# Reordering the first retention segment and splitting a mask-table load in a fused retention and SwiGLU kernel

## The chip, the cores and the metric

The kernel runs on one core of a Trainium2 chip. The metric is device time in microseconds (us) for one execution, given as the median of several runs. A core has a matmul engine (PE, its weight loads are PEld), a vector engine (DVE), a scalar engine (ACT), a Pool engine (POOL) and a queue engine (SP) that here issues all the DMAs. Each engine works through its own list of instructions in the order in which the program gives them, and semaphores make one engine wait for another.

## The reference

A retention layer is followed by a SwiGLU feed-forward block. There are 4 sequences of 768 positions, 8 heads, and 64 columns to a head.

```
state = gamma[h] * state + outer(k[t], v[t])        # for each sequence and head
y[t]  = scale * q[t] @ state
x     = y with heads side by side                    # 3072 x 512
out   = (silu(x @ w_gate) * (x @ w_val)) @ w_out     # 512 -> 1536 -> 512
```

The weights arrive in double precision and are turned into single precision on the chip.

## The kernel before, in words

The retention is computed in chunks of 128 positions. Inside a chunk, the scores k.q are multiplied by a table of decays (the mask) and then by v; what came earlier enters through a small state matrix. Four segments of 768 tokens each (three chunks of two sequences) pass through the feed-forward block: an up stage of 12 column blocks f (products with the gate and value weights, arranged as seven products of half-size blocks instead of eight), then a down stage.

The first segment is special. Its retention (six chunks, numbered 0 to 5 in the order in which they are handled) is the first thing that the kernel does, and it happens while the first weights are loaded and converted. The order of this part is written out by hand in a string, START (line 291), and `do` (line 284) walks through it: each word calls one helper, and each helper appends instructions to the lists of the engines that it uses. A word is a letter, a chunk or piece number, and sometimes a part:

- `l n:w` loads array w (0 is k transposed, 1 is q transposed, 2 is v, 3 is k) of chunk n, 256 KB (line 143). `A n` loads a part of the table of masks and decays (line 277; the parts are in `tabs`, line 977).
- `s n` makes the scores of chunk n on PE into banks 4 and 5 (line 418), and then multiplies them by the mask on DVE into a buffer (line 424). All six chunks use these two banks, so the scores of one chunk wait until the mask operations of the one before have read them.
- `k n`, `q n` scale k and q by decays on POOL (lines 437 and 432); capital `K n`, `Q n` do it on DVE.
- `t n` is the state product on PE (line 458), followed by a copy on ACT (line 461) or an addition on DVE (line 463). `g n` decays a state on ACT (line 444).
- `m n` mixes: products of q with the state (line 475) and of the masked scores with v (line 478) on PE, and a copy to `first` on ACT (line 481). Chunks 0 and 1 have no state yet and so only the second half.
- `x j:i` are sums of pairs of chunk outputs on DVE (line 80, called from line 633), needed by the seven-product scheme. `T n:i` are the corresponding sums of weights.
- `w n` issues n products of zeros on PE (line 963), whose result nobody reads.
- `U n:p` loads weight piece n in double precision, 1 MB for a pair of gate and value blocks (line 191), into the staging buffer `rawp` number p/2. `a n`, `b n`, `c n` are the three ACT parts of its conversion (lines 209, 213, 217), `S n` the DVE part (line 223), `C n` the POOL part (line 232), which frees the staging buffer. Piece 0 has its POOL part in two halves.

A DMA that must wait (for its buffer, or for the landing of the DMA eight places before it) waits on SP, and all DMAs behind it in the list wait with it. Two such waits matter here. U2 goes into the buffer of piece 0 and has to wait for C0. U3 goes into the buffer that holds k and q of chunk 5, so it has to wait for q5, and for m5 on PE.

After START, `up(f)` (line 653) issues the seven products of a block (line 663), with a list `beside` of further conversions between them. The down stages follow, `h_split` (line 851) taking its offsets from a table WHEN. Segments 1 to 3 take their products from lines 824 and 874.

Of the kernel before, what the change touches and what calls it, by code (L numbers as in the profile page):

```python
# [24 lines left out]
NF = DFF // P  # L25
# [10 lines left out]
MASK0, QDEC0, KDEC0, GDEC0 = 0, 2 * NP * P, 3 * NP * P, 3 * NP * P + H  # L36
NTAB = GDEC0 + NP
# [12 lines left out]
def tile_retnet_swiglu(  # L50
# [69 lines left out]
    def at(t, fn, *args, **kw):  # L120
        events.append((t, len(events), lambda: fn(*args, **kw)))
# [23 lines left out]
    def seg_chunks(s):  # L145
        p, pos = divmod(s * L, NCK)
        return [(2 * p + i) * NCK + pos + j for j in range(L) for i in range(2)]
# [136 lines left out]
    def do(order):  # L284
# [4 lines left out]


    START = """
        l0:0 l0:1 A0 l1:0 l1:1 l0:2 l1:2 A1 l0:3 l2:0 l2:1 l1:3 l2:2 l2:3 l3:0 l3:1 l3:2
        l3:3 l4:0 l4:1 U0:0 l4:2 l5:0 l5:1 l5:2 l4:3 l5:3 s1 s0 K0 m1 w6 k2 K1 t0 m0 s2 t1
        g3 Q2 g2 x0:0 x0:1 s3 U1:2 q3 m2 m3 t2 x1:0 k3 a0 x0:2 x0:3 t3 b0 x1:1 s4 S0 q4 x1:2
        c0 s5 q5 x1:3 m4 C0 m5 a1 x2:0 U3:4 T0:0 x2:1 T0:1 U2:0 T0:2 x2:2 x2:3 U12:6
    """
    beside = """
        b1 | c1 S1 U13:7 | g5 g4 C1 | a2 T1:0 U14:8 | U15:9 | c2 b2 T1:1 a3 |
# [26 lines left out]
    WHEN = {  # L325
        ('u', 0): (1.15, 2.19, 2.89, 3.24, 4.29, 5.33, 6.38, 7.08, 7.43, 8.13),
        ('u', 1): (1.15, 2.19, 2.89, 3.24, 4.29, 5.33, 6.38, 7.08, 7.43, 8.13),
        ('u', 2): (1.15, 2.19, 2.89, 3.24, 4.29, 5.33, 6.38, 7.08, 7.43, 8.13),
        ('u', 3): (1.15, 2.19, 2.89, 3.24, 4.29, 5.33, 6.38, 7.08, 7.43, 8.13),
        ('w', 0, 0): (-9.0, -7.4, -6.2),  # L330
        ('w', 0, 1): (-9.0, -7.4, -6.2),
        ('w', 0, 2): (-9.0, -7.4, -6.2),
        ('w', 1, 0): (-7.2, -5.6, -4.4),
# [14 lines left out]
        ('h', 9): (-7.5, -6.3, -5.3),  # L348
        ('h', 10): (-7.5, -6.3, -5.3),
        ('h', 11): (-7.5, -6.3, -5.3),  # L350
        ('s', 0, 0): (0.0, 0.0),
        ('s', 0, 1): (0.0, 0.0, 0.0, 0.0),
        ('m', 0): (0.0, 0.0, 0.0),
# [31 lines left out]
    UP0, T0 = 9.45, 18.0  # L385
# [323 lines left out]
    def item(kind, n):  # L709
        k = turns[kind]  # L710
        turns[kind] += 1
        slots = {"g": 4, "o": 3}[kind]
        t = place(f"{kind}item{k}", {"g": 3 * 2 * TH, "o": 3 * DM}[kind], R12,
                  tag=f"{kind}{k % slots}")
        return t[:, : 3 * n].rearrange("p (a b) -> p a b", a=3)

    def near_a(o, x):
        act(o[0], x, AF.Copy, scale=CUT / FAR)  # L718

    def near_b(o, x):  # L720
        stt(o[1], f32(o[0]), -FAR, x, op0=mul, op1=add)  # L721

    def near_c(o, op=pool):
        op(o[2], f32(o[0]), f32(o[1]), op=add)  # L724
# [52 lines left out]
    def make_x(t, s, p):  # L777
        for m, d in enumerate(WHEN["sum", p]):
            at(t + d, sum_x, m)
        for n in range(3):  # L780
            for d, step in zip(WHEN["far", p, n], (
                    lambda n=n: far_a(*x_part(s, p, n)), lambda n=n: far_b(*x_part(s, p, n)),
                    lambda n=n: far_c(x_part(s, p, n)[0]), lambda n=n: far_d(x_part(s, p, n)[0]))):
                at(t + d, step)
# [63 lines left out]

    hs, wo = {}, {}

    def h_split(t, f):
        it = {}

        def begin():
            hs[f] = item("g", 2 * TH)
            it["o"] = [hs[f][:, i] for i in range(3)]
            near_a(it["o"], hT[:, f].rearrange("p i t -> p (i t)"))

        a, b, c = WHEN["h", f]
        at(t + a, begin)  # L860
        at(t + b, lambda: near_b(it["o"], hT[:, f].rearrange("p i t -> p (i t)")))
        at(t + c, lambda: near_c(it["o"], both))

    def w_load(t, f):
        def load():
            wo[f] = item("o", DM)
            nc.sync.dma_start(out=wo[f].bitcast(U32), in_=w_dn3[f])

        at(t - 8.0, load)
# [31 lines left out]
    def down_stage(s, t, first_order=range(6), between=None):  # L901
        nxt = s + 1 if s + 1 < NSEG else None
        slot_at, steps = [], []
        for n in range(6 * NF):
            f, b = divmod(n, 6)
            slot_at.append(t)
            if b == 0:
                steps.append(t)
            if nxt and n in PARTS:
                what, p, g = PARTS[n]  # L910
                ci = seg_chunks(nxt)[2 * p] % NCK
                d = t + COST[what] + 0.1
                if what == "s":
                    at(t, scores_of, p, g)
                    w = WHEN["s", p, g]
                    for i in range(2):
                        at(d + w[i], decayed, p, g, i)
                    if g and ci:
                        for i in range(2):
                            at(d + w[2 + i], scale_q2, p, i)  # L920
                elif what == "m":
                    at(t, mix_own, nxt, p)
                    w = WHEN["m", p]
                    at(d + w[0], fence)
                    if ci < NCK - 1:
                        for i in range(2):
                            at(d + w[1 + i], scale_k2, p, i)
                elif what == "o":
                    at(t, mix_other, nxt, p)
                    if p == 0:  # L930
                        at(t, begin_x, nxt)
                    for k, w in enumerate(WHEN["y", p]):
                        at(d + w, bring_y, k % 2, k // 2 % 2, k // 4)
                    if ci < NCK - 1:
                        at(d + WHEN["old", p], decay2, nxt, p)
                    make_x(d, nxt, p)
                elif ci < NCK - 1:
                    at(t, state2, nxt, p)
                    at(d + WHEN["new", p], keep_state, nxt, p)
                t += COST[what]  # L940
            tok = (first_order if f == 0 else range(6))[b]
            at(t, down, f, tok)
            t += 3 * PASS_D
            if f == NF - 1:
                at(t + WHEN["end" if nxt else "last"][tok], finish, s, tok)
            if between and n == 0:
                at(t, between)
                t += 1.0
        for f in range(NF):
            h_split(steps[f], f)  # L950
            if s or f > 2:
                w_load(steps[f], f)
        if nxt:
            for n, h in LOADS.items():
                at(slot_at[h] + 1.0, load_pair, nxt, n)
            for f in range(3):
                at(slot_at[UNITS[f]], load_unit, f)
        return t
# [15 lines left out]
    early = [flat[:, ts(i, 512)] for i in range(18)] + [  # L974
        hsp[:, ts(i % 4, 512)] for i in range(6)]

    tabs = slice(0, QDEC0), slice(QDEC0, NTAB)
    early[20:22] = early[18:20]
    early[18:20] = [chunk_x[:, ts(i, 512)] for i in (2, 3)]
    early[22:] = [chunk_x[:, ts(i, 512)] for i in (0, 1)]  # L980
# [8 lines left out]
    for n in range(3, 5):  # L989
        at(end + 1.0 + n, load_pair, 1, n)  # L990
    t = down_stage(0, end, (0, 4, 3, 2, 5, 1), last_gates)
    for s in range(1, NSEG):
        for f in range(NF):
            up3(s, f, t + UPT * f)
            if f > 2:
                at(t + UPT * (f - 1) - 2.5, load_unit, f)
        t += NF * UPT
        if s + 1 < NSEG:
            for n in range(5):
                at(t - (18, 13, 12, 5, 4)[n], load_pair, s + 1, n)  # L1000
        t = down_stage(s, t)
# [52 lines left out]
```

## Time and profile before

| | before |
|---|---|
| runs (us) | 695.98, 696.91, 695.15; median 695.98 |
| the profiled execution, its own time | 693.57 us |
| its span | 691.8 us |
| PE busy from 0 to 9.03 us | 3.78 us |
| PE busy from 14.50 to 36.57 us (retention) | 20.27 of 22.07 us |
| PE busy from 36.57 to 86.15 us (up stage, first part) | 46.36 of 49.58 us |
| PE busy from 86.15 to 150.00 us (up stage, the rest) | 63.85 of 63.85 us |
| the rest, 150.00 to 691.80 us | 527.16 of 541.80 us |

The profile is of one execution, so its times are held against 693.57 us and not against the median. Its span is 1.8 us shorter than the time. A line of the timeline gives start and duration in us, the engine, the line of the kernel, the operation, what it writes and reads, and a count; in brackets stands the idle time of the engine before it and what ended it. A matmul in single precision shows as two instructions, so the 8 products of a chunk's scores are "x16".

### The profile page before, as it was taken

The page shows a single profiled execution, that of the slowest core. Times are in us where ns is not written, and L with a number is a line of the kernel's source. Part 1 is how long each engine was busy: PE and PEld are TensorE (multiplying, and loading weights), DVE is VectorE, ACT ScalarE, POOL GpSimd, SP SyncE. Part 2 cuts the span into 40 slices and gives each one's busy share as a digit, 9 for nine tenths or more (in the row PEclk, how much of TensorE's full clock was granted, in tenths as well). Part 3 has the DMA queues.
Part 4 walks back from the last instruction along what each step waited for, and adds up shares of the span by engine and source line. Part 5 has one row for each costly group of instructions (what it writes and reads, how often), then busy time and mean ns, then how long its engine had stood idle before and what let it go on. Part 6 is the DMA issues. An engine that isn't in the chain of part 4 may idle for free.

```text
span 691.8 us, 12321 instructions
## 1 busy us (share of the span) xinstructions
PE 666.2 (96%) x4724; PEld 551.0 (80%) x4724; DVE 474.9 (69%) x742; ACT 382.5 (55%) x793; POOL 250.3 (36%) x164
## 2 busy tenths in 40 slices
PE   6899899999999999999999999999999999999997
PEld 5755455567678899997777899998777799999885
DVE  2558998985887766665777767666577867667541
ACT  1488879755556454553578555554464645555111
POOL 0334557640112666640110665661011465562000
PEclk9999999999999999999999999999999999999999
DMA  8689899966574543364756433264756453313553
GB/s 316 230 309 335 313 328 400 397 226 216 202 253 169 196 146 107 132 217 162 249 203 220 170 137 116 98 205 168 232 180 213 194 190 126 140 54 119 196 188 136
DMA packets 49578, 141.58 MB, mean 205 GB/s; under 512 B 6128, under 2 KB 18928, under 8 KB 49520
## 3 DMA queue, kind: packets, MB, share of 16 engines
q1 hardware_dynamic: 49520, 140.80, 58.6%
q8 instruction: 37, 0.61, 0.3%
q14 instruction: 21, 0.17, 0.1%
HBM read 114.04 MB, written 26.74 MB: 204 GB/s over the span
## 4 chain that ended last, share of the span: by engine, by line
PE 64%; DVE 17%; ACT 9%; issue 4%; DMA 3%; SPq 1%; POOL 0%; DVEq 0%; ACTq 0%; POOLq 0%
PE bank L824 34%; PE bank L874 14%; PE bank L663 9%; PE bank L520 4%; ACT chunk_x L759 4%; DVE gitem L721 3%; DVE x L733 2%; DVE x L80 2%; DMA rawp<-in_w_gate_dram 2%; DVE tmp L80 1%; DVE gitem L80 1%; PE bank L418 1%; ACT gitem L718 1%; DVE chunk_x L885 1%; DVE tmp L539 1%
## 5 line engine op out<-in xcount | busy, mean ns | idle before, releaser
L824 PE MATMUL bank<-x,gitem 128*128 128x384 f32 x1296 | 233.7, 336 | 3.8 <-ACT tmp L840 3.8
L824 PEld LDWEIGHTS bank<-x,gitem 128*128 128x128 f32 x1296 | 225.6, 188 | 6.9 <-ACT tmp L840 5.7
L874 PE MATMUL bank<-oitem,gitem 128*128 128x512 f32 x864 | 214.5, 401 | 0.0
L874 PEld LDWEIGHTS bank<-oitem,gitem 128*128 128x128 f32 x864 | 158.8, 188 | 40.3 <-issue 2.9
L724 POOL TENSOR_TENSOR gitem<-gitem 128x768 fp32r<-128x768 f32 x72 | 136.1, 1890 | 132.4 <-DVE gitem L721 132.4
L721 DVE SCALAR_TENSOR_TENSOR gitem<-gitem,loads 128x768 fp32r<-128x768 f32 x72 | 74.1, 1029 | 62.8 <-ACT gitem L718 62.8
L663 PE MATMUL bank<-first 128*128 128x384 f32 x336 | 110.9, 489 | 3.2 <-DVE hT L696 2.2
L663 PEld LDWEIGHTS bank<-first 128*128 128x128 f32 x336 | 62.8, 190 | 49.4 <-DVE hT L696 3.1
L721 DVE SCALAR_TENSOR_TENSOR gitem<-gitem,hT 128x768 fp32r<-128x768 f32 x48 | 46.2, 963 | 46.7 <-ACT gitem L718 46.4
L593 POOL TENSOR_TENSOR loads<-loads,tab 128x512 f32<-128x512 f32 x8 | 15.0, 1879 | 156.5 <-PE bank L520 156.5
L718 ACT ACTIVATE gitem<-loads 128x768 fp32r<-128x768 f32 x72 | 60.8, 844 | 0.0
L843 ACT ACTIVATE bank<-bank 128x384 f32<-128x384 f32 x36 | 17.1, 475 | 78.3 <-PE bank L824 78.3
L718 ACT ACTIVATE gitem<-hT 128x768 fp32r<-128x768 f32 x48 | 39.6, 838 | 25.9 <-PE bank L874 25.8
L232 POOL TENSOR_TENSOR first<-first,rawp 128x1024 int32<-128x1024 int32 (+1 forms) x21 | 41.4, 1975 | 34.4 <-DVE first L223 17.9
L80 DVE SCALAR_TENSOR_TENSOR gitem<-gitem 128x768 fp32r<-128x768 f32 x48 | 45.8, 954 | 1.0
L759 ACT COPY chunk_x<-bank 64x256 f32<-64x256 f32 x72 | 26.5, 368 | 35.6 <-PE bank L520 33.6
L824 PE MATMUL bank<-x,oitem 128*128 128x384 f32 x216 | 44.0, 339 | 1.3 <-DVE hT L841 1.3
L840 ACT ACTIVATE bank<-tmp 128x384 f32<-128x384 f32 x36 | 17.8, 496 | 48.1 <-DVE tmp L839 48.1
L739 ACT ACTIVATE x<-x 128x512 fp32r<-128x512 f32 (+2 forms) x27 | 18.9, 700 | 37.8 <-DVE x L733 37.8
L824 PEld LDWEIGHTS bank<-x,oitem 128*128 128x128 f32 x216 | 36.8, 188 | 3.2 <-DVE hT L841 2.3
L724 POOL TENSOR_TENSOR oitem<-oitem 128x256 fp32r<-128x256 f32 x36 | 28.6, 794 | 15.2 <-DVE oitem L721 13.5
L520 PEld LDWEIGHTS bank<-loads 64*64 64x64 f32 (+1 forms) x800 | 22.6, 134 | 13.8 <-issue 5.1
(93 smaller groups left out, 738.3 us busy)
## 6 DMA issues: line engine op xcount, KB each, us to landing
oitem<-wdnt SPq DMA_DIRECT2D x45, 768.0 KB, 4.3
loads<-wup SPq DMA_DIRECT2D x36, 896.0 KB, 4.7
wup<-first SPq DMA_DIRECT2D x12, 896.0 KB, 7.4
wdnt<-oitem SPq DMA_DIRECT2D x12, 768.0 KB, 5.5
rawp<-in_w_val_dram SPq DMA_DIRECT2D x24, 256.0 KB, 5.5
rawp<-in_w_gate_dram SPq DMA_DIRECT2D x12, 512.0 KB, 6.5
out_dram<-chunk_x SPq DMA_DIRECT2D x24, 256.0 KB, 2.1
loads<-in_k_t_dram SPq DMA_DIRECT2D x18, 256.0 KB, 4.4
```

The source lines that it names most:

```text
L80: stt(o, x, 1.0, y, op0=mul, op1=op)
L232: pool(d[:, ts(i, n)].bitcast(I32), d[:, ts(i, n)].bitcast(I32), lo[:, ts(i, n)].bitcast(I32), op=add)
L520: nc.tensor.matmul(o, a, b, start=start, stop=True, skip_group_check=True)
L663: nc.tensor.matmul(o, w[:, slot, k], a[:, k], start=(start and k == 0), stop=(stop and k == KH - 1), skip_group_check=True)
L718: act(o[0], x, AF.Copy, scale=CUT / FAR)
L721: stt(o[1], f32(o[0]), -FAR, x, op0=mul, op1=add)
L724: op(o[2], f32(o[0]), f32(o[1]), op=add)
L739: act(o[2], f32(o[2]), AF.Copy, scale=FAR / ONE)
L759: copy(cx[half[i], ds(2 * h, 2), c], y_both(h, i, c))
L824: nc.tensor.matmul(o, w[:, a, k], xs_of[s][:, a, OP[p], k], start=start and a == k == 0, stop=a == 2 and k == KH - 1, skip_group_check=True)
L840: lambda: act(gate, c11, AF.Silu, scale=ONE), lambda: copy(u2, x),
L874: nc.tensor.matmul(banks[tok], hs[f][:, a, ds(i * TH + u * P, P)], wo[f][:, a], start=f == a == 0, stop=f == NF - 1 and a == 2, skip_group ...
```

## The change

START is put in another order, the table is loaded in three parts instead of two (the masks in two halves of 256 KB, then the rest), and `h_split` gets an index of its own into WHEN.

```
     START = """
-        l0:0 l0:1 A0 l1:0 l1:1 l0:2 l1:2 A1 l0:3 l2:0 l2:1 l1:3 l2:2 l2:3 l3:0 l3:1 l3:2
-        l3:3 l4:0 l4:1 U0:0 l4:2 l5:0 l5:1 l5:2 l4:3 l5:3 s1 s0 K0 m1 w6 k2 K1 t0 m0 s2 t1
-        g3 Q2 g2 x0:0 x0:1 s3 U1:2 q3 m2 m3 t2 x1:0 k3 a0 x0:2 x0:3 t3 b0 x1:1 s4 S0 q4 x1:2
-        c0 s5 q5 x1:3 m4 C0 m5 a1 x2:0 U3:4 T0:0 x2:1 T0:1 U2:0 T0:2 x2:2 x2:3 U12:6
+        l0:0 l0:1 A0 A1 l1:0 l1:1 l0:2 l1:2 A2 l0:3 l2:0 l2:1 l1:3 l2:2 l2:3 l3:0 l3:1 l3:2
+        l3:3 l4:0 l4:1 U0:0 l4:2 l5:0 l5:1 l5:2 U1:2 l4:3 l5:3 s0 w6 s1 m0 m1 K0 t0 K1 s2 t1
+        g2 g3 Q2 s3 m2 x0:0 x0:1 x0:2 x0:3 k2 q3 t2 s4 a0 b0 m3 k3 t3 q4 c0 s5 S0 x1:0 x1:1
+        x1:2 x1:3 m4 a1 q5 C0 U2:0 m5 x2:0 T0:0 x2:1 T0:1 x2:2 x2:3 T0:2 U3:4 U12:6
     """
...
         ('h', 11): (-7.5, -6.3, -5.3),
+        ('h', 12): (-7.5, -6.3, -5.3),
...
-    def h_split(t, f):
+    def h_split(t, f, when):
...
-        a, b, c = WHEN["h", f]
+        a, b, c = WHEN["h", when]
...
-            h_split(steps[f], f)
+            h_split(steps[f], f, f if nxt else NF)
...
-    tabs = slice(0, QDEC0), slice(QDEC0, NTAB)
+    tabs = slice(0, QDEC0 // 2), slice(QDEC0 // 2, QDEC0), slice(QDEC0, NTAB)
```

The moves, in words: the scores of chunk 0 come ahead of those of chunk 1 and so do the mixes; the six products of zeros move from behind m1 to between s0 and s1; U1 moves ahead of the loads of k for chunks 4 and 5; U2 moves ahead of U3; m3 moves behind s4 on PE; a0 and b0 move ahead of the copy of m3 on ACT, a1 ahead of the copy of m5; x0 is finished before the states and masks that follow it on DVE, x1 starts behind S0; q4, k3 and k2 change places with their neighbours on POOL. The number of instructions is the same but for one more DMA.

## The prediction

> **What bounds the kernel now.** I read the page first, then the chain of waits up to 170 us, then the timeline of the first 40 us, then the DMA view of the first 60 us. The page says that PE is the engine to watch, and that only the start is thin.
>
> ```profile
> PE 666.2 (96%) x4724; PEld 551.0 (80%) x4724; DVE 474.9 (69%) x742; ACT 382.5 (55%) x793; POOL 250.3 (36%) x164
> ...
> PE   6899899999999999999999999999999999999997
> ```
>
> The chain of waits (start, duration, what) names what sets the end of the up stage:
>
> ```profile
> 2.59 6.30 DMA hT<-in_q_t_dram
> ...
> 9.03 2.10 PE bank L418 x16
> ...
> 34.60 1.05 PE bank L475 x16
> ...
> 38.20 6.42 DMA rawp<-in_w_gate_dram
> ...
> 48.79 2.52 POOL first L232
> ...
> 53.89 7.18 DMA rawp<-in_w_gate_dram
> ...
> 86.15 44.50 PE bank L663 x136
> ```
>
> Read backwards: from 86.15 us PE is full. Before that the chain runs through the conversion of weights: the load of piece 4 (landing at 53.89 + 7.18 = 61.07), behind C2 on POOL, behind the load of U2 (landing at 44.62), behind U3, which stood on SP until m5. Above all that is q of chunk 1, landing at 8.89. So both the PE queue and the weight queue hang on the end of the retention. The timeline shows its pieces:
>
> ```profile
> 1.05 3.78 PE L963 MATMUL bank<-warm 128*128 128x128 f32 x16 [1.05 <-DVE warm L967]
> ...
> 9.03 2.08 PE L418 MATMUL bank<-hT 64*128 64x128 f32 x16 [4.20 <-DMA hT<-in_q_t_dram]
> ```
> ```profile
> 27.67 1.16 ACT L209 ACTIVATE first<-rawp 128x1024 f32<-128x1024 f32 x1
> ...
> 32.58 3.48 SPq L191 DMA_DIRECT2D rawp<-in_w_val_dram  x2
> ...
> 36.57 1.56 PE L663 MATMUL bank<-first 128*128 128x384 f32 x4
> ```
>
> PE stands idle 4.20 us for chunk 1, although k and q of chunk 0, issued at 0.74 and 1.19, land 2.7 and 2.8 us later, by 4.0. Piece 0 lands at 22.0 (its gate half issued at 15.67, 6.3 to landing), but ACT takes it up at 27.67. U3 holds SP for 3.48 us.
>
> **What the Trainium skill says.** "TensorE: Matmul & The Clock Gate", Part 1: The HAM clock gate: matmuls run at half the clock until about 3.4 us of sustained work, and again after an idle window of that length. The trace agrees: 16 products of zeros take 3.78 us at the start (0.236 each) and 12 take 1.60 at 16.34 us (0.133 each); scores take 2.08 us at 9.03, after the 4.20 us gap, and 1.09 to 1.16 from 19.36 on. "DMA: Bandwidth & Descriptors", Anatomy of one DMA: a semaphore wait happens on the issuing sequencer before dispatch, so what stands behind it waits too. The trace agrees: the second DMA of U3 went at 35.66, as m5's state half ended (35.64), and U2 only at 37.19.
>
> **The change part by part.**
>
> *Half table.* One more issue on SP, 0.42 us by the row of the table's first part. Transfers are the limit at that point (256 KB land every 0.66 us, 388 GB/s), so landings move by 0 to 0.42 us; I take 0.2. Mask 0 lands at about 6.4 and mask 1 at 7.55, where before the whole landed at 7.55.
>
> *PE up to s3.* I walk each engine's list, with durations of the rows. s0 starts when the zeros end, 4.87, and takes 2.08 cold: 6.95. The six products of zeros: 12 x 0.236 = 2.84 cold: 9.8. This is cover for the wait for chunk 1 (landing 8.9 to 9.3). Masks of s0 on DVE: 6.95 to 8.35, so banks 4 and 5 are free. s1 at 9.8 at the latest, warm (PE has worked 8.7 us without a gap): 1.15, to 10.9 (before, the second scores ended at 14.52). m0 1.02: 11.9. m1 needs the masks of s1 (10.9 + 1.29 = 12.2): to 13.2. K0 on DVE 0.95: 13.15; t0 0.65: 13.85. s2 (q landed 13.0): 15.0. K1 needs k of chunk 1 (13.65), then 0.95; t1 to 15.65. s3 needs the masks of s2 (15.0 + 1.29 = 16.3) and q of chunk 3 (landing 10.94 + 5.4 = 16.35): 16.4 to 17.5. Before, s3 started at 21.30.
>
> *s3 to m5.* m2 2.05: 19.6 (Q2 done by 17.0). t2: 20.2. s4 1.15: 21.4. m3 2.05: 23.4 (q3 on POOL, 17.5 + 1.28, done by 18.9). t3: 24.1. s5 needs q of chunk 5, landing 17.70 + 6.7 = 24.4: to 25.6. m4 2.05 (q4 on POOL done by 22.7): 27.65. m5 2.05 (q5 25.65 + 1.28 = 26.9, masks of s5 26.9): **29.7**, against 36.57. So the landing of chunk 5 sets it, with some 0.4 us to spare in what comes before.
>
> *First weights.* On ACT, m2's copy ends at 20.2, so a0 takes piece 0 at about 22.1 (it landed at 22.0): 1.16, b0 1.12, so 24.4. S0 stands behind the masks of s5 on DVE: 26.9 + 1.28 = 28.2. C0 on POOL, two halves of 1.27: 30.8, against 36.40. U1, two loads of 256 KB further forward, lands 1.3 us earlier, at 27.9; a1 at 28.3 to 29.5; copy of m5 29.75 to 30.35; first x2 sum 30.8; first weight sum T0 behind C0, 0.68: 31.5. The first product of the up stage runs 29.75 to 31.05 under that (or, if it waits for all of C0, 30.85 to 32.15); the second starts at **31.55**, against 38.38 before: 6.8 us earlier.
>
> *Second weights.* U2 goes at 30.9, not at 37.19; ahead of U3 it lands within about 4.7 us (1 MB at 390 GB/s is 2.7, and 2 for the landing): 35.6, against 44.62. But on ACT it stands behind the copies of the first block and the eight decays of g4 (41.77 + 2.01 = 43.8 before, so 37.0 now): a2 gains only 0.9 us beyond the 6.8. U3, now second, lands about 38.4; a3 was taken up at 47.84, hence now at 41.0, so its loss of place is hidden by 2.6 us. If C0 came later, U2 and U3 would both be later by as much.
>
> *Do the transfers follow?* By the DMA view, the rate fell to nothing from 28.5 to 33 us, and from 33 to 39 it was (134 + 52 + 89 + 150)/4 = 106 GB/s; as full rate, the restart was at 37.3. Now it is about 31.8 (30.9 and 0.9 to the first bytes, as at the start): 5.5 us earlier. To the end of piece 4 it has U2, U3, four pieces of w_out (2 MB), two stores (1.8 MB), U5 and U4: 7.8 MB, 20.6 us at 380. Before: 37.3 + 20.6 + 1.6 = 59.5, against a landing at 61.07, so 1.6 us of slack. Now: 54.0; through C2: 61.07 - 6.8 - 0.9 = 53.4. The later is 54.0, a shift of 7.1. So the gap of 2.24 us ahead of 86.15 stays or loses 0.3. I count 0.
>
> *Nothing:* the index of `h_split` reads equal numbers. x0 and x1 in other places cost DVE the same instructions, with cover by m2 to m5. The loads of k for chunks 4 and 5 come 1 MB (2.6 us) later, but their users stand among the last blocks of the up stage.
>
> Sum: -6.8 + 0.2 = -6.6 us. From 86 us on all is relative to PE, so it carries to the end. Profiled execution: 693.57 - 6.6 = 687.0. The median of the runs shown is 2.4 above it: 695.98 - 6.6 = **689.4**.
>
> **The rivals.**
>
> *Partly given back in the up stage (15%).* Pieces 2 to 5 don't follow the retention: if U2 and U3 come 2 to 4 us later than I think (C0 behind on POOL, or the transfers more bound), the gap ahead of 86.15 grows by as much. For it: ACT is busy 9.77 of 10 us from 60 to 70, and DVE 9.64 from 80 to 90. Against: both have over 2 us idle in each of the earlier tens. Time: 695.98 - 6.6 + 3 = 692.4.
>
> *Hand-offs bind (8%).* The retention is bound by DVE, ACT and POOL handing over, not by landings, and saves only what s0 and s1 save: 14.52 - 10.9 = 3.6, less about 0.5 of new waits. Time: 692.9. Against: PE was busy 20.27 of 22.07 us from 14.50 on.
>
> *It does nothing (6%).* The weights come at the same absolute time, as if bound by transfers from the start, and the gain at 31 us turns into wait at 86. Time: 696.0. Against: the idle DMA from 28.5 to 33.
>
> *Slower: the clock goes cold (6%).* The zeros stood at 16.3 in front of the long run of products; now they are used up at 9.8, and PE waits in short gaps from 11.9 to 16.4. From s1 to m5 there are 18.6 us of warm work (5 x 1.15, 10 x 1.02, 4 x 0.65). Cold, by 2.08 against 1.15, it is 34: 9.8 + 34 = 43.8, 7.2 later than 36.57. Time: 703.2. It is slower once over half of that work is cold (36.57 - 9.8 - 18.6 = 8.2 us of 15.4). Against: no gap is over 1.3 us, and the clock held through gaps of 0.97.
>
> **How the numbers follow.** Forecast 65%, rivals 15, 8, 6 and 6%. The forecast's own span runs from -8.5 (cold part shorter, the 0.9 kept, the gap of 2.24 partly gone) to -5 (C0's wait, landings 0.4 later, 5.5 by the transfers alone): 687.5 to 691.0. The range reaches to the two part-way cases: 687.3 to 693.2; it leaves out the last two and the tail. 0.3% of the time, 2.1 us, is about what a measurement here can tell from no change: faster 0.87, same 0.07, slower 0.06.
>
> **What would show it.** s0 starting near 4.9 and s1 ending by 11; s5 waiting for a landing near 24.4; the first product of line 663 near 30 and its second near 31.6; U2 issued near 31; PE full from about 79. Wrong: scores still at 2 us after 12 us, C0 ending after 33, or a gap of over 3 us near 79.

## The result, and the profile after

| | before | changed |
|---|---|---|
| median of the runs beside each other (us) | 695.77 (4 runs) | 689.84 (4 runs) |
| the same on another chip, later | 694.73 (36 runs) | 690.72 (6 runs) |
| the profiled execution, its own time | 693.57 | 690.12 |
| its span | 691.8 | 688.3 |

The ratio is 0.9914, with a 95% interval of 0.9891 to 0.9937, so the change takes 4.4 to 7.6 us off; on the second chip it is 0.9942 (0.9927 to 0.9957), 3.0 to 5.1 us. Forecast were 689.4 us and a gain of 6.6. Two executions on that chip lay far above the rest at a low clock and count in no median here: a 37th of before (817.68) and the profiled one of the kernel called e10 (932.81), whose profile is not read.

The page of the changed kernel, in the lines shown of before:

```profile
PE 664.9 (97%) x4724; PEld 549.4 (80%) x4724; DVE 475.5 (69%) x742; ACT 382.2 (56%) x793; POOL 250.5 (36%) x164
...
PE   8898899999999999999999999999999999999997
```

The first two slices of PE rose from 6 and 8 to 8 and 8, and the fourth (51.6 to 68.8 us) fell from 9 to 8: the work is the same, most of the hole at the start is filled, and there is a smaller new one. The timeline of the start (start, duration, engine, line; in brackets the wait ahead of it):

```profile
4.77 2.04 PE L419 MATMUL bank<-hT 64*128 64x128 f32 x16
...
6.74 1.60 PE L964 MATMUL bank<-warm 128*128 128x128 f32 x12
...
8.38 1.16 PE L419 MATMUL bank<-hT 64*128 64x128 f32 x16
...
15.73 1.16 PE L419 MATMUL bank<-hT 64*128 64x128 f32 x16 [1.28 <-DMA hT<-in_q_t_dram]
```
```profile
24.42 1.16 PE L419 MATMUL bank<-rawp 64*128 64x128 f32 x16 [1.36 <-DMA rawp<-in_q_t_dram]
...
29.61 1.56 PE L664 MATMUL bank<-first 128*128 128x384 f32 x4
...
31.53 26.38 PE L664 MATMUL bank<-first 128*128 128x384 f32 x80 [0.37 <-DVE first L80]
...
59.58 4.14 PE L664 MATMUL bank<-first 128*128 128x384 f32 x12 [1.67 <-DVE hT L697]
```

Scores of chunk 0 start at 4.77, as soon as the zeros are through; the two long waits that are left in the retention (1.28 and 1.36 us) both end with the landing of a chunk. The second product of the up stage starts at 31.53 where it was 38.39: 6.86 us earlier. Then there is a wait at 59.58 that the kernel before didn't have. The lists of ACT and DVE say where it comes from. The first two lines are of the changed kernel, the third of before:

```profile
55.97 1.14 ACT L209 ACTIVATE first<-rawp 128x1024 f32<-128x1024 f32 x1 [2.17 <-DMA rawp<-in_w_gate_dram]
...
57.77 1.28 DVE L223 SCALAR_TENSOR_TENSOR first<-first,bank 128x512 uint32<-128x512 uint32 x2 [2.35 <-ACT bank L213]
```
```profile
61.20 1.16 ACT L209 ACTIVATE first<-rawp 128x1024 f32<-128x1024 f32 x1
```

On DVE, the operation that PE waits for (line 697) stands behind the DVE part of piece 4, which waits for ACT, which waits 2.17 us for piece 4 to land. Before, ACT came to piece 4 just as it landed (its operation ahead of it ended at 61.06) and did not wait. The chain of waits goes further back:

```profile
31.71 5.62 DMA rawp<-in_w_gate_dram
...
41.51 2.52 POOL first L232
...
47.66 8.14 DMA rawp<-in_w_gate_dram
...
80.84 46.18 PE bank L664 x136
```

It is the same chain as before: piece 2, POOL's step C2, piece 4, and the run of 136 products. Piece 2 lands at 37.33 (44.62 before), C2 ends at 44.03 (51.31), each 7.3 earlier. But the six loads of pieces 5 and 4 take 3.6 us to issue instead of 2.6, piece 4 takes 8.14 us from its last issue instead of 7.18, and it lands at 55.80, only 5.27 earlier; the run of 136 products starts 5.31 earlier. From the landing of piece 4 to that start is 25.0 to 25.1 us in both kernels. And in both the DMA engines are busy all the way to that landing (columns: length, busy time of PE, PEld, DVE, ACT and POOL, the granted clock, the share and the rate in GB/s of the DMA engines; the first line is of the changed kernel, the second of before):

```profile
31.70:55.80 24.10, 24.10 (x74) 13.82 (x75) 16.86 (x32) 18.28 (x36) 10.24 (x5) 1.00 1.01 369
```
```profile
38.20:61.07 22.87, 22.26 (x68) 12.86 (x69) 16.04 (x31) 18.78 (x38) 8.99 (x4) 1.00 1.00 365
```

The run of 136 products takes 46.18 us, and 44.50 before. The same view shows why:

```profile
81.70:85.10 3.40, 3.40 (x7) 1.74 (x6) 2.69 (x6) 0.88 (x2) 2.99 (x2) 0.51 0.74 211
85.10:90.00 4.90, 4.90 (x16) 2.85 (x15) 2.39 (x5) 3.12 (x5) 1.82 (x2) 1.00 0.98 302
```

PE ran 3.4 us at half its clock, just after a wait of 2.25 us: 1.7 us lost in this run. The kernel before had a wait of 2.24 us at the same place and kept its clock. So in the two profiled executions 6.86 us were won by 31 us, 1.5 given back by 81 and 1.7 more by 128 (131.20 against 127.56).

### The profile page after: what moved, and what is told of

The parts are those of the page before. It is cut to its first block, busy times and chain, and to the rows that moved or that the text cites. A ratio compares the mean times of both kernels' runs of the same rounds, so it can differ in the third digit from the quotient of the medians.

```text
span 688.3 us, 12325 instructions
## 1 busy us (share of the span) xinstructions
PE 664.9 (97%) x4724; PEld 549.4 (80%) x4724; DVE 475.5 (69%) x742; ACT 382.2 (56%) x793; POOL 250.5 (36%) x164
## 4 chain that ended last, share of the span: by engine, by line
PE 62%; DVE 17%; ACT 9%; DMA 5%; issue 4%; SPq 1%; POOL 0%; DVEq 0%; ACTq 0%; POOLq 0%
PE bank L825 34%; PE bank L875 14%; PE bank L664 10%; PE bank L521 4%; ACT chunk_x L760 4%; DVE gitem L722 3%; DVE x L734 2%; DVE x L80 2%; DMA rawp<-in_w_gate_dram 2%; DVE tmp L80 1%; DVE gitem L80 1%; ACT gitem L719 1%; DVE chunk_x L886 1%; DVE tmp L540 1%; DMA rawp<-in_q_t_dram 1%
## 5 line engine op out<-in xcount | busy, mean ns | idle before, releaser
L664 PE MATMUL bank<-first 128*128 128x384 f32 x336 | 112.9, 495 | 4.6 <-DVE hT L697 3.9
L664 PEld LDWEIGHTS bank<-first 128*128 128x128 f32 x336 | 63.4, 192 | 52.2 <-DVE hT L697 5.1
```

The source lines that it names most:

```text
L664: nc.tensor.matmul(o, w[:, slot, k], a[:, k], start=(start and k == 0), stop=(stop and k == KH - 1), skip_group_check=True)
```

## The experiments

Landmarks from the trace of each, in us. "Second" is the start of the up stage's second product, "piece 4" is the time at which ACT takes up piece 4, "run" the start of the products after the wait on line 696 (697 in the changed kernel) that ends last. The medians come from three sets of runs: the median of before beside them was 695.46 for e1 to e4, 694.68 for e5 to e8 and 694.73 for e9 to e12, so a time is best compared by its ratio to before.

| kernel | second | piece 4 | run | median |
|---|---|---|---|---|
| before | 38.39 | 61.20 | 86.15 | 695.77, 694.73 |
| changed | 31.53 | 55.97 | 80.84 | 689.84 |
| e1 no zeros | 31.44 | 56.77 | 81.64 | 690.57 |
| e2 whole table | 31.43 | 56.24 | 81.11 | 690.34 |
| e3 old queue of weights | 33.09 | 55.28 | 80.20 | 688.51 |
| e4 scores first only | 35.06 | 57.80 | 81.75 | 691.05 |
| e5 late w_out | 31.16 | 54.17 | 80.01 | 689.92 |
| e6 old queue, late w_out | 32.04 | 54.61 | 79.52 | 689.78 |
| e7 reorder only | 35.08 | 59.30 | 84.30 | 693.56 |
| e9 1 MB more | 31.41 | 58.86 | 85.31 | 693.02 |
| e11 changed again | 31.31 | 56.05 | 80.92 | 690.72 |
| e12 piece 3 first | 34.30 | 58.33 | 83.25 | 687.86 |

The theory: the retention is bound by the landings of chunks, so the change wins what PE lost waiting for chunk 1; in the up stage the transfers of weights bind, and give part of it back. Its rivals: hand-offs between engines or the clock bind the retention; the order of the conversions binds the up stage.

**e1: without the zeros.**

```
-    ... s0 w6 s1 m0 m1 ...
+    ... s0 s1 m0 m1 ...
```

> The changed kernel without the six products of zeros between the scores of chunks 0 and 1 (their result is read by nobody). Landings theory: the landing of chunk 5 (24.3 us) sets the scores of chunk 5, and PE has 1.28 + 1.36 us of waits for landings ahead of it, so even a colder clock costs at most 0.5 us at the second product of the up stage (31.53 us). Clock theory: without them PE goes back to the slow clock in the gap before the scores of chunk 1; scores of chunk 1 take 2.0 us and not 1.16, the mixes 1.9 and not 1.02, and the second product of the up stage comes over 1 us later.

Measured: scores of chunk 1 at 8.15 us in 1.23 us, second product 31.44, median 690.57 (ratio to before 0.9931, 0.9913 to 0.9949). The clock had turned by itself. In this place the zeros are worth nothing that can be measured.

**e2: the table in one load.**

```
-    l0:0 l0:1 A0 A1 l1:0 l1:1 l0:2 l1:2 A2 ...
+    l0:0 l0:1 A0 l1:0 l1:1 l0:2 l1:2 A1 ...
```

> The changed kernel with the table of masks in one load of 512 KB as before. Landings theory: the first mask operation waits for about 7.5 us instead of starting at 6.84, the scores of chunk 1 start near 8.9 instead of 8.38, and PE's wait of 1.28 us before the scores of chunk 3 takes that up: second product of the up stage at 31.5, time within 0.3 us. Rival, the half table is what lets chunk 0 go first: the 0.5 to 1 us is handed on to the up stage.

Measured: scores of chunk 1 wait 1.03 us for the first mask and start at 8.59; chunk 3 at 15.98, second product at 31.43; 690.34 us (0.9933, 0.9913 to 0.9952). Chunk 3 still waits (1.31 us); it is the wait for the landing of chunk 5 that takes it up (1.07 us and not 1.36). The half table is worth nothing that can be measured either.

**e3: pieces 1 to 3 in their old places on SP.**

```
-    ... l5:2 U1:2 l4:3 l5:3 ...   ... C0 U2:0 m5 ... T0:2 U3:4 U12:6
+    ... l5:2 l4:3 l5:3 U1:2 ...   ... C0 m5 x2:0 U3:4 ... T0:1 U2:0 ... U12:6
```

> The changed kernel with the loads of weight pieces 1, 2 and 3 in their old places (piece 1 behind both loads of k, piece 3 ahead of piece 2). Transfers theory: what counts is how early the DMA engines start again; piece 3 goes near 29 us, so they start some 1.5 us earlier than now, piece 4 lands at or before 55.8 us, and the gap of 1.67 us at 59.6 us is no larger. Conversion theory: what counts is piece 2, which lands near 38.5 and not 37.3; POOL frees its buffer 1.2 us later, piece 4 lands near 57, and the gap grows to about 2.7 us. Both: piece 1 lands 1.3 us later, the second product of the up stage at 31.5 to 32.1.

Measured: the first 256 KB of piece 3 go at 25.83 and the rest from 28.93 on, piece 2 at 30.98. The second product is late (33.09: PE waits 1.72 us, since a1 for the later piece 1 stands ahead of the copy of m5 on ACT), and piece 2 lands later (38.14 and not 37.33), as does the end of C2 (44.96 and not 44.03). Still piece 4 is taken up 0.7 us earlier than in the changed kernel and the wait at 59.6 is gone. So it is the transfers, not piece 2. Median 688.51 (0.9901, 0.9881 to 0.9921); the time alone would not tell it from the changed kernel, whose interval overlaps.

**e4: the kernel before with only the scores of chunk 0 first, the zeros behind them and the half table.**

```
-    ... s1 s0 K0 m1 w6 k2 K1 t0 m0 s2 t1 ...
+    ... s0 w6 s1 K0 m0 m1 k2 K1 t0 s2 t1 ...
```

> The kernel before with only what the few words of the change say: the table in halves, scores of chunk 0 first with the zeros behind them, then chunk 1; every later word of the hand-written order as before. Landings theory: the rest of the retention follows the landings, up stage's second product at 31.5 to 32.5 us (38.38 before), total 4 to 5.5 us under the kernel before. Hand-offs theory: the old order of DVE, ACT and POOL keeps its intervals, second product near 34.5, total about 3 us under it.

```profile
16.99 1.16 PE L418 MATMUL bank<-hT 64*128 64x128 f32 x16 [2.47 <-DVE first L80]
```

Measured: second product at 35.06, 3.3 us earlier than before and 3.5 later than in the changed kernel; up to 1.7 of that is a half-clock window from 18.6 to 22.0. Here the scores of chunk 3 wait 2.47 us for DVE, which in the old order does x sums ahead of masks. So hand-offs do bind without the later words. But the total is 691.05 (0.9934, 0.9913 to 0.9956), only 1.2 above the changed kernel and not clear of it: of the 3.5 us that the later words win at the second product, 1.8 are left at piece 4 and 0.9 at the run.

**e5: two loads of w_out moved behind piece 4.**

```
-    ... a2 T1:0 U14:8 | U15:9 | ...   F12:0 U4:2 Z2
+    ... a2 T1:0 | | ...               F12:0 U4:2 U14:8 U15:9 Z2
```

> The changed kernel with two loads of w_out (pieces 14 and 15, 1 MB together, not needed before the fourth block) moved on SP from ahead of the first stores to behind the load of piece 4. Transfers theory: piece 4 lands about 2.6 us earlier (1 MB at 380 GB/s), near 53.2 and not 55.8; PE's wait of 1.67 us at 59.6 is gone; the run of 136 products starts 25.0 us after that landing, near 78.2 and not 80.84. Conversion theory: piece 4 waits for POOL, ACT and DVE through piece 2, its landing moves by under 0.5 us and both waits stay.

```profile
57.79 4.14 PE L664 MATMUL bank<-first 128*128 128x384 f32 x12 [0.39 <-DVE hT L697]
63.19 14.58 PE L664 MATMUL bank<-first 128*128 128x384 f32 x44 [1.26 <-ACT tmp L688]
80.01 32.75 PE L664 MATMUL bank<-first 128*128 128x384 f32 x100 [2.24 <-DVE hT L697]
114.94 11.88 PE L664 MATMUL bank<-first 128*128 128x384 f32 x36 [2.18 <-ACT tmp L691]
```

Measured: piece 4 is 1.8 us earlier, not 2.6, and the wait of 1.67 us shrinks to 0.39, as the transfers theory has it. But the time stays: a wait of 1.26 us comes at 63.19, where ACT's copy stands behind a conversion that waits 0.87 us for the load of piece 6, and one of 2.18 us at 114.94, behind an ACT step that waits for a transfer. 689.92 us (0.9930, 0.9905 to 0.9954). The hole was moved, not filled.

**e6: the same move on top of e3.**

> The same move of pieces 14 and 15, in the kernel that has the loads of pieces 1, 2 and 3 in their old places. Transfers theory: piece 4 lands near 52.8 (2.5 us earlier than 55.3), the run of 136 products starts near 77.8 (80.20 without the move), the time falls by another 1 to 2.5 us to about 686.5. Conversion theory: nothing over 0.5 us.

Measured: piece 4 at 54.61, the run at 79.52, with waits of 1.31 us at 63.68 and 1.75 at 114.02 in exchange; 689.78 us (0.9932, 0.9908 to 0.9956), not 686.5. A miss: the earlier landing of one piece did not shorten the time here. That the transfers as a whole are late, and so turn up at another piece, is how I read e5 and e6 together.

**e7: all of the change but what its few words say.**

```
-    ... s0 w6 s1 m0 m1 K0 t0 K1 s2 t1 ...
+    ... s1 s0 K0 m1 w6 K1 t0 m0 s2 t1 ...     (and the table in one load)
```

> The changed kernel without what its few words say: the table in one load, scores of chunk 1 first and then chunk 0, zeros behind the first mix as before; all later words as in the changed kernel. Landings theory (chunk 0 first is worth what PE waits for chunk 1): scores of chunk 3 near 19.9 and not 15.73, the second product of the up stage near 35 and not 31.5, the run of 136 products near 84, time about 3 us over the changed kernel. Rival, the later words do it: second product under 32.5, time within 1 us of the changed kernel.

```profile
8.12 1.83 PE L419 MATMUL bank<-hT 64*128 64x128 f32 x16 [3.28 <-DMA hT<-in_q_t_dram]
10.66 2.67 PE L419 MATMUL bank<-hT 64*128 64x128 f32 x16 [0.71 <-DVE tmp L425]
...
35.08 5.11 PE L664 MATMUL bank<-first 128*128 128x384 f32 x15 [0.39 <-DVE first L80]
```

Measured: second product 35.08 and run 84.30, as the landings theory had them (35 and 84), and 693.56 us (0.9987, 0.9977 to 0.9998). Without chunk 0 first, the rest of the reordering is worth 0.1 to 1.6 us. With e4: each half alone leaves the second product at 35.1 (e4 at 33.4 by estimate, without the 1.7 us of its half-clock window), both together bring it to 31.5.

**e8: the kernel before, a second profile.**

> The kernel before, for a second profile, since its profiled execution (693.57 us) lies 2.4 us under its median. Clock theory: the difference is windows of half clock on PE (3.4 us each, costing 1.7 us each), which this profile shows at the wait near 86 us or at the late waits of the retention in later segments; outside them every landmark is within 0.3 us. Rival: the waits themselves are longer, with a full clock.

Measured: 696.11 us, span 694.3. PE ran at half clock from 7.9 to 18.2 (in the first profile its products were slow until 16.3), and the first product of the up stage came at 37.11 instead of 36.57. But waits are longer too: 1.22 us at 50.73 (0.43 at 49.40 in the first profile) and 0.49 at 120.45. So both theories are true in part, and the first profile of before was one of its better executions: only 3 of the 36 on the other chip were faster.

**e9 and e10: 1 MB more to transfer,** loaded once more from w_out ahead of the other loads of w_out, in the changed kernel and in the kernel before.

```
+    def extra_load(n):
+        for i in range(2):
+            nc.sync.dma_start(out=spare[:, i], in_=w_out[ts(n + i, P)].bitcast(U32))
...
-    ... T0:2 U3:4 U12:6
+    ... T0:2 U3:4 D0 U12:6
```

> The changed kernel with 1 MB of w_out loaded once more, into memory that nobody reads, on SP behind piece 3 and ahead of the other loads of w_out: work added, nothing of the result changed. If transfers bind the up stage: piece 4 lands 2.6 us later (58.4 and not 55.8), the run of 136 products starts near 83.5, and the end of the up stage and the time are 2 to 3 us later. If they don't (the slack of 1.6 us that the prediction gave them): piece 4 lands 1 us later at most, the time is within 1 us.

> The kernel before with the same 1 MB more, ahead of the loads of w_out. By the prediction's step, transfers had 1.6 us of slack ahead of piece 4 in the kernel before: it lands 1.0 us later (62.1 and not 61.07) and the run of 136 products starts near 87.2. Without slack: it lands 2.6 us later (63.7), the run starts near 88.8.

```profile
62.46 20.90 PE L671 MATMUL bank<-first 128*128 128x384 f32 x56 [4.97 <-DVE hT L704]
```

Measured, e9: piece 4 is taken up at 58.86, 2.9 us later, the wait of 1.67 us grows to 4.97 (its kernel has seven lines more, so L671 is L664), and the time is 693.02 against 690.72 (e11, same chip): 2.3 us for 1 MB. e10: 696.80 against 694.73, 2.1 us; ratio 1.0028 (1.0018 to 1.0039), so 1.3 to 2.7 us. A slack of 1.6 us would have let through 1.0. The up stage was bound by its transfers before the change, too, or had at most 1.3 us to spare. In e10 this rests on the time alone; where piece 4 landed was not seen.

**e11 and e12: the changed kernel again, and with piece 3 alone back ahead of piece 2.**

```
-    ... C0 U2:0 m5 x2:0 T0:0 x2:1 T0:1 x2:2 x2:3 T0:2 U3:4 U12:6
+    ... C0 m5 x2:0 U3:4 T0:0 x2:1 T0:1 U2:0 x2:2 x2:3 T0:2 U12:6
```

> The changed kernel once more, beside the next one on the same chip, and for a second profile. Second product of the up stage at 31.5 us and the landing of piece 4 near 55.8 as before; if the half-clock window of 3.4 us at 81.7 us is by chance of its phase, it is elsewhere or absent and the run of 136 products takes 44.5 us and not 46.2, with a wait near 115 us in its place if the weights bind there.

> The changed kernel with only piece 3 back ahead of piece 2 on SP (piece 1 stays ahead of the loads of k). Transfers theory: piece 3 goes at 28.7 us, so the engines start 1.5 to 2 us earlier; second product still at 31.5, piece 4 lands by 55.0, the time falls 0.5 to 1.5 us below the changed kernel. Conversion theory (piece 2 first is what helps): piece 2 lands 1 us later, piece 4 lands after 56.5, the time is 0.5 to 1 us above it.

Measured, e11: the landmarks of the table within 0.3 us of the first profile (the scores of chunks 1 and 3 come 0.7 us later, and a shorter wait ahead of chunk 5 takes that up); no half-clock window, the run of products without the loss, and in its place a wait of 0.53 us at 114.19. Its profiled execution took 689.77 us. e12: median 687.86 (0.9916, 0.9890 to 0.9942), 2.9 us under e11 by the medians, though the intervals overlap. Its profiled execution was its slowest (692.71), and shows what the clock can do (columns as above):

```profile
17.20 2.08 PE L419 MATMUL bank<-hT 64*128 64x128 f32 x16 [2.74 <-DMA hT<-in_q_t_dram]
```
```profile
16.30:23.10 6.80, 5.90 (x54) 5.38 (x56) 2.79 (x6) 0.48 (x2) 2.27 (x2) 0.50 1.07 369
23.10:34.00 10.90, 10.80 (x164) 8.68 (x162) 6.99 (x14) 6.68 (x10) 5.10 (x4) 1.00 0.61 197
```

A wait of 2.74 us for chunk 3, then 6.8 us at half clock: scores 2.08 us, mixes 1.97. The second product came at 34.30. A second stretch of 3.4 us followed the wait ahead of the run, as in the profiles of e1 and e3. Three of the five other executions, with a mean clock of 1.00, took 687.1 to 687.3 us; two executions of the changed kernel at that clock took 688.76 and 690.17, so the clock does not explain the gain. Where it lies was not seen in a profile at full clock; e3's profile shows 0.64 us of it at the run.

## Why the prediction was right, and which term was off

- *PE up to m5.* Right, step by step: scores of chunk 0 at 4.77 (forecast 4.87), of chunk 1 ending at 9.54 (10.9 at the latest), of chunk 3 starting at 15.73 (16.4), of chunk 5 at 24.42 (24.4), the first product at 29.61 (29.7), the second at 31.53 (31.55). The landing of chunk 5 sets it; e7 shows that this hangs on chunk 0 coming first, e4 that the later words are needed as well. The spare time was 1.36 us, not 0.4. It is a near tie, though: in e11, the same kernel, PE waited 0.56 us there, and the wait ended with an addition to a state on DVE (line 464) and not with the landing.
- *The zeros and the half table.* The zeros were called cover and the table cost 0.2. Neither could be measured (e1, e2).
- *First weights.* C0 ended at 30.75 (30.8), U2 was issued at 30.78 (30.9).
- *Second weights.* Piece 2 landed at 37.33, not at 35.6; C2 ended 7.3 us earlier and not 7.7. The loss of place of piece 3 was called hidden. ACT did take piece 3 up at 40.57, as forecast (41.0). But the order is not free: the DMA engines stand still until U2 is issued at 30.78, while in e3 the first part of piece 3 went at 25.83 and the rest from 28.93 on.
- *Do the transfers follow?* This is the term that was mis-sized. I gave the transfers 1.6 us of slack ahead of piece 4 in the kernel before, and so let its landing move by 7.1. It moved by 5.27, about as far as the restart of the engines (5.5 by my own figure). The sum of volumes at 380 GB/s was good to 2 us in 20, and the slack was within that. Two terms of it were off or open: up to the landing 8.9 MB went through and not 7.8 (24.10 us at 369 GB/s in the changed kernel), and both sums hold 1.6 us for which the prediction gives no reason. With the DMA engines at a share of 1.00 in the kernel before there was no slack to hand on; e9 and e10 show that 1 MB costs 2.3 and 2.1 us. So 1.5 us of the 6.8 came back as the wait at 59.58. This is the first rival, in half its size, and not at the gap that it named.
- *The gap ahead of 86.15.* It stayed, 2.25 us, as counted. What was not counted is that such a gap can cost a half-clock window.
- *Carried to the end.* Up to 81 us 5.3 were left, and in the profiled executions 3.5 (e11: 3.8) at the end. The medians give 4.0 to 5.9, because the profiled execution of before was a good one (e8). The forecast of 6.6 was 0.7 to 2.6 too much, inside its range. That the median came within 0.4 us of 689.4 is in part luck: the profiled execution was put at 687.0 and took 690.12.
- *Hand-offs bind:* wrong for the change, right for half of it (e4). *It does nothing:* wrong. *The clock goes cold:* not in the retention of the changed kernel's two profiles (the window at 81.7 is later), but in one execution of e12, where a wait for chunk 3 was 2.74 us and not 1.28; the late landing and the clock together cost 2.8 us at the second product. I had it as a rival by the Trainium skill, "TensorE: Matmul & The Clock Gate", Part 1: The HAM clock gate, which asks for an idle window of about 3.4 us; here waits of 2.25 and 2.74 us were enough where they fell within one step of the clock (see the last section). The profile of before shows no return to half clock after its gap of 4.20 us, as its clock had not come up before 16.3; e8 shows it, with full clock from 4.5 to 7.9 and then half. And the gap of 0.97 us in the argument against was one of the weight loads; the products' own was 0.78.

## What to carry to other kernels

Work that is moved forward wins only up to the next thing that does not move with it: before counting a gain to the end, ask for each queue that feeds the later stage how much earlier it restarts, and give it no slack that is smaller than the error of the estimate. How busy its DMA engines are in that stretch (here a share of 1.00, on record before the change) says more than a sum of volumes. To see whether transfers bind a stage, add a known amount and read the landing; to see whether one load binds it, move that load: here the first cost 2.1 to 2.3 us per MB, and the second moved the wait without shortening the time. An early half and a late half of a reordering can each be worth little alone.

## What the hardware did that I had not expected

- Half-clock stretches of PE come in multiples of 3.41 us (3.4 in the changed kernel, 6.8 in e12, 10.2 in e8) and may follow a wait of 2.25 us, or not, in the same kernel (the changed kernel and e11). The traces show what it goes with: in each, the clock changes only on steps of 3.41 us counted from its first change, and a change to half clock follows a step in which PE was little busy. The first line is the step of the changed kernel that holds the wait, the other two are the steps over which it is divided in e11 (columns as above):

```profile
78.32:81.73 3.41, 1.16 (x4) 0.63 (x4) 3.38 (x5) 1.54 (x4) 1.57 (x1) 1.00 1.02 414
```
```profile
76.15:79.56 3.41, 2.52 (x8) 1.08 (x6) 3.38 (x7) 2.78 (x5) 1.04 (x1) 1.00 0.85 346
79.56:82.97 3.41, 2.05 (x7) 1.26 (x8) 3.41 (x7) 1.46 (x4) 1.33 (x2) 1.00 1.04 407
```

- In the thirteen profiles, each of the 15 steps at full clock in which PE was busy for less than 1.43 us was followed by half clock, and none of some 2,560 with 1.70 us or more; of the six between, two were. So a wait of 2.25 us is harmless or not by where it falls on the steps.
- Such a stretch costs PE 1.7 us, but not always the time: it hides the wait of 0.53 us near 114 us that e11 has, and the products after the run start only 1.0 us later (127.56 against 126.61).
- Which execution gets them differs, and with it the time: the six executions of e12 took 687.1 to 692.7 us. A single profiled pair (3.5 us apart) said less about this change than its runs did (4.0 to 5.9).
- Between ACT taking up piece 4 and the start of the run lie 24.9 to 25.0 us in ten of the thirteen profiles read (the kernels of the table, and e8), whatever happened ahead of it; the three others are e4 (23.95), e5 (25.84) and e9 (26.45).
